# Writing the order of a feed-forward stage by hand: single steps on four engines, and some twenty turns of attention and mixing moved

## The chip, the cores and the metric

The kernel runs on one core of one Trainium2 chip. Times are device microseconds (us) of that core from launch to end. Five engines work side by side, each through its own instructions in a fixed order: TensorE (PE; its weight loads, PEld, are listed apart), VectorE (DVE), ScalarE (ACT), GpSimd (POOL), and SyncE (SP), which here only starts transfers (DMA). An instruction waits at the head of its engine's queue until what it reads has been written and the buffer that it writes is free; all that stands behind it on that engine waits with it.

## The reference, cut to what matters

```python
# attention: 8 heads, 768 tokens, head size 64; a key counts only where its hash bucket equals the query's
scores = where(q_bucket == k_bucket, q @ k.T / 8, -1e9)
x = concat_heads(softmax(scores) @ v)                    # 768 x 512
# gated feed-forward with a mixing over the tokens
h = gelu_tanh(x @ w_in)                                  # 768 x 1024
u, v = h[:, :512], h[:, 512:]
v_n = (v - mean(v)) / sqrt(var(v) + 1e-6) * g_ln
gated = u * (w_sg @ v_n + b_sg[:, None])
x = x + gated @ w_out
# eight experts, one per token (argmax of x @ w_gate, or the expert of the token before)
out[s] = p[e] * (relu(x[s] @ w1[e]) @ w2[e])
```

## The kernel before, in words

Tokens are cut into six tiles of 128. A product in full float32 is made from two halves of each factor, a rounded one ("hi") and the rest ("lo"): hi is cast by ACT or DVE, lo is a subtraction on DVE or POOL, and TensorE takes three products (hi hi, hi lo, lo hi).

**Attention** runs over the heads; the table ATTENTION writes the order of its steps for PE, DVE, ACT and POOL. `score h t` makes the scores of one query tile, `max` their row maximum (DVE, L384), `exp` the numerators (ACT, L388), `turn h i` three transposes of them into one of two PSUM banks (PE, L396), `ev h i` the copy out of that bank (ACT, L400), `pv` the product with v (PE, L410). `prep h ...` scales and splits q and k of the head two further on: `k1` is a cast (DVE, L339), `q2` a scaling (DVE, L337), `k2` a subtraction (POOL, L349). `out`, `to_x` bring a head's result to x: three transposes into bank "m" and a DVE multiplication out of it (L445). The same bank "m" takes `project` (PE, L361), which makes the hash bits of the next head. `conv` is the next of the small steps that turn w_in and w_out into hi and lo (DVE L237 to L250, a cast on ACT L256, POOL or DVE L229). `to_x 5` handles the head that the code counts as 3, since `to_x h` works on head h-2.

**Feed-forward, first stage.** h = x @ w_in comes in twelve PSUM banks: (n, t) with n = 1 for the v half and n = 0 for the u half, t the tile. Four of them (hv0 to hv3) have three quarters of their products inside the attention table. Each bank goes through gelu: Square on ACT (L641), a cubic term on DVE (L642), Tanh on ACT (L643), a product on DVE (L644). A v bank goes on: mean (DVE, L653), squared deviation (ACT, L654), z (DVE, L656), variance (DVE, L657), its power -1/2 on POOL (L658), scaling of z by it (ACT, L659), cast to hi (DVE, L660), lo (POOL, L661). Beside that stand the first two of six tiles of w_sg: a transfer, a cast on ACT (L673, `wshi`), a subtraction on POOL (L675, `wslo`).

Before, only PE's order was written out here (in the order of the code). DVE, ACT and POOL were put in order by the compiler's scheduler from its own costs.

**Mixing** follows from the table MIXING, again for four engines: `mix t k` is the k-th of 18 products of w_sg tile t with v_n, `gated t` the product with u (DVE, L686), `gT t` its transposes (PE, L692), `out t k` the product with w_out, `route t` the steps that pick experts, `w` the next step of the split of the first expert weights (ACT L614, then DVE or POOL L618). Then the **experts** run, with 4 MB of weights each; their raw buffers are six of 0.5 MB, loaded by SP as soon as one is free.

Of the kernel before, what the change touches and what calls it, by code (L numbers as in the profile page):

```python
# [67 lines left out]
turn 4 5, ev 4 5, score 4 4, max 4 4, conv 0, exp 4 4, conv 0, zero 0 4, conv 0 *3, pv 3 1, pv 3 2, turn 4 6,  # L68
ev 4 6, turn 4 7, ev 4 7, score 4 5, max 4 5, exp 4 5, project 4 1, bits 4 2, bits 4 3, sum 4 3, pv 3 3, turn 4 8,
ev 4 8, turn 4 9, ev 4 9, prep 4 k1, prep 4 k2, prep 4 hi, score 5 0, max 5 0, exp 5 0, pv 3 4, pv 3 5, turn 4 10,  # L70
ev 4 10, turn 4 11, ev 4 11, out 4, conv 0 *3, prep 4 q2, sum 5 1, prep 4 lo, fetch 5, xT 4, score 5 1, max 5 1,
exp 5 1, mean 5, low 4, turn 5 0, ev 5 0, turn 5 1, ev 5 1, score 5 2, max 5 2, exp 5 2, sum 5 0, pv 4 0,
conv 0 *4, to_x 5, turn 5 2, ev 5 2, turn 5 3, ev 5 3, score 5 3, max 5 3, exp 5 3, project 5 0, bits 5 0,
bits 5 1, pv 4 1, turn 5 4, ev 5 4, turn 5 5, ev 5 5, score 5 4, max 5 4, exp 5 4, pv 4 2, conv 0 *2, sum 5 2,
zero 0 5, turn 5 6, ev 5 6, sum 5 3, conv 0, turn 5 7, ev 5 7, score 5 5, max 5 5, exp 5 5, project 5 1, bits 5 2,
pv 4 3, turn 5 8, ev 5 8, turn 5 9, ev 5 9, score 6 0, prep 5 k1, prep 5 k2, prep 5 hi, conv 0 *2, max 6 0,
exp 6 0, pv 4 4, pv 4 5, turn 5 10, ev 5 10, turn 5 11, mean 6, ev 5 11, out 5, sum 6 0, bits 5 3, xT 5, prep 5 q2,
prep 5 lo, score 6 1, conv 0, max 6 1, low 5, exp 6 1, turn 6 0, ev 6 0, turn 6 1, ev 6 1, score 6 2, max 6 2,
exp 6 2, conv 0 *3, pv 5 0, to_x 6, sum 6 1, turn 6 2, ev 6 2, turn 6 3, ev 6 3, score 6 3, max 6 3, exp 6 3,
conv 0, pv 5 1, project 6 0, bits 6 0, bits 6 1, conv 0, turn 6 4, ev 6 4, turn 6 5, ev 6 5, sum 6 2, score 6 4,  # L80
max 6 4, exp 6 4, pv 5 2, zero 0 6, conv 0 *2, project 6 1, bits 6 2, turn 6 6, ev 6 6, turn 6 7, ev 6 7, conv 0,
score 6 5, max 6 5, exp 6 5, conv 0, bits 6 3, pv 5 3, conv 0, turn 6 8, ev 6 8, turn 6 9, ev 6 9, score 7 0,
max 7 0, exp 7 0, conv 0 *3, sum 6 3, pv 5 4, pv 5 5, out 6, turn 6 10, ev 6 10, turn 6 11, ev 6 11, sum 7 2,
mean 7, xT 6, score 7 1, max 7 1, exp 7 1, low 6, sum 7 1, turn 7 0, ev 7 0, turn 7 1, ev 7 1, score 7 2, max 7 2,
exp 7 2, sum 7 0, pv 6 0, to_x 7, conv 0, turn 7 2, ev 7 2, turn 7 3, ev 7 3, score 7 3, max 7 3, exp 7 3, pv 6 1,
# [30 lines left out]
route 2, mix 5 10, mix 5 11, route 3, mix 5 12, route 2, w 0, half 2 1, mix 5 13, gl 4, mix 5 14, route 3 *2,
mix 5 15, route 3, mix 5 16, mix 5 17, route 3, out 4 0, route 2, out 4 1, route 2, half 3 0, route 2, route 3,
out 4 2, out 4 3, out 4 4, route 3, out 4 5, out 4 6, gated 5, w 0, out 4 7, route 3 *3, out 4 8, out 4 9, w 0,
out 4 10, route 3, out 4 11, res 4, gT 5, route 3 *2, half 3 1, route 3 *2, gl 5, w 0, route 3, route 4,
route 3 *6, out 5 0, out 5 1, out 5 2, w 0, out 5 3, route 3, out 5 4, route 4, route 3, out 5 5, out 5 6, out 5 7,  # L120
route 4, out 5 8, w 0, route 4, w 0, route 4, out 5 9, out 5 10, route 4, out 5 11, res 5, gx 0 0, route 4 *2,
half 4 0, w 0, gx 0 1, route 4 *2, half 4 1, gx 1 1, gx 0 2, gx 0 3, route 5, route 4 *2, gx 1 0, gx 1 2, gx 1 3,
route 4 *2, route 5 *3, half 5 0, route 5, route 4, route 5, route 4, gx 2 0, gx 2 2, route 4, gx 2 1, route 5 *3,
w 0, route 4, route 5, route 4 *2, route 5, half 5 1, route 4 *2, route 5, gx 2 3, route 5, route 4, route 5,
route 4, gx 3 0, gx 4 0, route 4, gx 3 3, gx 4 3, gx 3 2, gx 4 2, gx 3 1, gx 4 1, route 5 *3, gx 5 0, gx 5 1,
# [20 lines left out]
def kernel(  # L146
# [480 lines left out]
    with ExitStack() as ctx_b:  # L627
# [11 lines left out]
        def gelu2(h_ps, dst, total=None):  # L639
            sq = bp2.tile([P, DM], F32, tag="sq", name="sq", bufs=3)  # L640
            nc.scalar.activation(sq, h_ps, AF.Square)  # L641
            nc.vector.scalar_tensor_tensor(sq, sq, 1.0 / A3, h_ps, op0=ALU.add, op1=ALU.mult)  # L642
            nc.scalar.activation(sq, sq, AF.Tanh, scale=CG * A3)  # L643
            nc.vector.scalar_tensor_tensor(dst, sq, 1.0, h_ps, op0=ALU.add, op1=ALU.mult, accum_out=total)  # L644
            return sq

        def v_part(t, h_ps):
            v2 = bp2.tile([P, DM], F32, tag="v2", name="v2")
            mu = bp2.tile([P, 1], F32, tag="mu", name="mu")
            var = bp2.tile([P, 1], F32, tag="var", name="var")  # L650
            rstd = bp2.tile([P, 1], F32, tag="rstd", name="rstd")
            sq = gelu2(h_ps, v2, mu)
            nc.vector.tensor_scalar_mul(mu, mu, -1.0 / DM)  # L653
            nc.scalar.activation(sq, v2, AF.Square, bias=mu, accum_out=var)  # L654
            z = bp2.tile([P, DM], F32, tag="z", name="z")
            nc.vector.scalar_tensor_tensor(z, v2, mu, gbc, op0=ALU.add, op1=ALU.mult)  # L656
            nc.vector.tensor_scalar(var, var, 1.0 / DM, 4e-6, op0=ALU.mult, op1=ALU.add)  # L657
            nc.gpsimd.tensor_tensor(rstd, var, eps4, op=ALU.pow)  # L658
            nc.scalar.activation(z, z, AF.Copy, scale=rstd)  # L659
            nc.vector.tensor_copy(vnh[:, t, :], z)  # L660
            nc.gpsimd.tensor_tensor(vnl[:, t, :], z, vnh[:, t, :].bitcast(F32), op=ALU.subtract)  # L661
# [548 lines left out]
```

## Time and profile before

| | us |
|---|---|
| median of 3 runs | 360.95 (359.12 to 362.23) |
| the profiled execution | 358.38 |
| its span | 356.6 |
| attention | 0 to about 155 |
| first feed-forward stage, first Square to last gelu | 156 to 191 |
| mixing and routing | to about 250 |
| experts | to 349 |

The profile shows one execution. An engine is busy while an instruction runs on it; idle time stands before the instruction that ended it, with the one that released it. "PEclk" is the share of full speed that the throttle granted TensorE. In the rows `out<-in` names what an instruction writes and reads.

### The profile page before, as it was taken

What the parts mean: (1) busy time and instruction counts of PE and PEld (TensorE: products, weight loads), DVE (VectorE), ACT (ScalarE), POOL (GpSimd) and SP (SyncE); (2) the same over time, 40 slices, a digit from 0 to 9 for tenths busy, and PEclk for the clock granted to TensorE, in tenths of its full rate; (3) what the DMA queues carried; (4) which work ended last, traced back from release to release, by engine and by line L of the source; (5) the groups of instructions that cost most, each with busy time, mean ns of one, the idle gap of its engine ahead of it and who ended that gap; (6) DMA issues with size and microseconds to landing.
All of it is one profiled execution on the core that took longest, in us unless ns stands there. A gap on an engine that the chain in (4) does not pass through costs nothing. (4 is left out here: it accounts for less than half of the span.)

```text
span 356.6 us, 5375 instructions
## 1 busy us (share of the span) xinstructions
PE 327.3 (92%) x1802; PEld 247.2 (69%) x1802; DVE 274.6 (77%) x553; ACT 233.2 (65%) x431; POOL 204.3 (57%) x172
## 2 busy tenths in 40 slices
PE   7678969999989999999986999997999999999990
PEld 5555546776656666688865777776888888888870
DVE  4799969887989977666875286788567989999570
ACT  3586667878868688346854465462668789978520
POOL 2457837747768534716742489597266455665351
PEclk9999999999999999999998999999999999999997
DMA  7695403213041103071012546456869999999400
GB/s 291 225 370 190 149 2 147 91 59 112 38 147 61 45 16 119 0 248 49 0 46 52 182 135 208 147 180 206 255 223 344 341 372 375 325 398 344 144 18 26
DMA packets 27535, 59.52 MB, mean 167 GB/s; under 512 B 3054, under 2 KB 7662, under 8 KB 27504
## 3 DMA queue, kind: packets, MB, share of 16 engines
q1 hardware_dynamic: 24912, 52.78, 43.5%
q0 software_dynamic: 1664, 4.74, 3.6%
q10 hardware_dynamic: 928, 1.62, 1.3%
q8 instruction: 16, 0.26, 0.3%
q14 instruction: 15, 0.12, 0.1%
HBM read 52.29 MB, written 7.36 MB: 167 GB/s over the span
## 5 line engine op out<-in xcount | busy, mean ns | idle before, releaser
L618 POOL TENSOR_TENSOR w<-raw,w 128x1024 fp32r<-128x1024 f32 x23 | 60.1, 2614 | 34.7 <-ACT w L614 34.7
L614 ACT CAST w<-raw 128x1024 fp32r<-128x1024 f32 x64 | 65.5, 1057 | 9.5 <-DMA raw<-in_w 7.7
L388 ACT ACTIVATE e<-s,nb_all 128x768 f32<-128x768 f32 x48 | 43.4, 905 | 31.6 <-DVE nb_all L384 30.8
L618 DVE TENSOR_TENSOR w<-raw,w 128x1024 fp32r<-128x1024 f32 x41 | 59.3, 1482 | 5.4 <-ACT w L614 4.4
L384 DVE TENSOR_REDUCE nb_all<-s 128x1 f32<-128x768 f32 x48 | 45.7, 953 | 11.9 <-PE s L380 11.5
L396 PEld LDWEIGHTS t<-ident,e 128*128 128x128 f32 x288 | 31.1, 140 | 27.7 <-ACT pt L400 16.9
L396 PE MATMUL t<-ident,e 128*128 128x128 f32 x288 | 42.3, 283 | 8.0 <-ACT pt L400 7.3
L400 ACT COPY pt<-t 128x384 f32<-128x384 f32 x96 | 41.2, 484 | 1.4 <-PE t L396 1.3
L410 PE MATMUL po<-pt,vt 128*64 128x384 f32 x192 | 38.1, 503 | 0.0
L968 PE MATMUL y<-w,hh 128*128 128x512 f32 x128 | 31.9, 397 | 0.4 <-DVE w L618 0.4
L377 PE MATMUL s<-k,q 128*128 128x384 f32 x96 | 28.4, 376 | 0.0
L968 PEld LDWEIGHTS y<-w,hh 128*128 128x128 f32 x128 | 23.4, 188 | 5.4 <-DVE w L618 0.8
L682 PE MATMUL vs<-vn,wshi 128*128 128x512 f32 x72 | 24.6, 417 | 1.2 <-POOL vn L661 0.9
L380 PE MATMUL s<-k,q 76*128 76x384 f32 x96 | 25.0, 342 | 0.4 <-DVE q L368 0.3
L675 POOL TENSOR_TENSOR wslo<-wsr,wshi 128x768 fp32r<-128x768 f32 x6 | 11.1, 1850 | 24.1 <-ACT wshi L673 19.2
L946 PE MATMUL eh<-w,xh 128*128 128x512 f32 x96 | 24.8, 400 | 0.0
L349 POOL TENSOR_TENSOR k<-r,k 64x768 fp32r<-64x768 f32 x7 | 13.8, 1972 | 19.1 <-DVE k L339 11.1
L270 PE MATMUL h<-w_in_s,xTs 128*128 128x512 f32 x96 | 21.9, 389 | 0.0
L410 PEld LDWEIGHTS po<-pt,vt 128*64 128x64 f32 x192 | 11.0, 135 | 14.3 <-issue 14.3
L229 POOL TENSOR_TENSOR cv_w<-cv_w,cv_a 128x512 f32<-128x512 f32 x11 | 14.3, 1299 | 11.4 <-DVE cv_w L241 11.2
L270 PEld LDWEIGHTS h<-w_in_s,xTs 128*128 128x128 f32 x96 | 18.0, 188 | 3.7
L946 PEld LDWEIGHTS eh<-w,xh 128*128 128x128 f32 x96 | 17.6, 188 | 3.8
(205 smaller groups left out, 720.2 us busy)
## 6 DMA issues: line engine op xcount, KB each, us to landing
raw<-in_w SPq DMA_DIRECT2D x64, 512.0 KB, 5.3
r<-in_qk SPq DMA_DIRECT2D x7, 768.0 KB, 4.5
raw<-in_w_in SPq DMA_DIRECT2D x8, 512.0 KB, 4.6
slots<-zt SPq DMA_DIRECT2D x7, 514.0 KB, 7.4
wsr<-in_w_sgT SPq DMA_DIRECT2D x6, 384.0 KB, 3.5
raw<-in_w_out SPq DMA_DIRECT2D x4, 512.0 KB, 3.5
xg<-slots POOLq DMA_DIRECT2D x6, 257.0 KB, 4.8
vt<-in_v_tok ACTq DMA_DIRECT2D x1, 1536.0 KB, 6.6
```

The source lines that it names most:

```text
L270: nc.tensor.matmul(ps, a[:, kc, ts_], w_in_s[:, b, kc, ns], start=(kc == 0 and i == 0), stop=(kc == 3 and i == 2))
L377: nc.tensor.matmul(s[:, j, :HALF], q1[:, ts_], k1[:, j * HALF:(j + 1) * HALF], start=True, stop=False)
L380: nc.tensor.matmul(s[:, j, :HALF], q2[:NB, ts_], k2[:NB, j * HALF:(j + 1) * HALF], start=False, stop=True)
L384: nc.vector.tensor_reduce(nb_all[:, h, t:t + 1], ss[h, t][:, :, :HALF], axis=AX.XY, op=ALU.max, negate=True)
L388: nc.scalar.activation(e, ss.pop((h, t))[:, :, :HALF], AF.Exp, bias=nb_all[:, h, t:t + 1], accum_out=rs_all[:, h, t:t + 1])
L396: nc.tensor.transpose(ps[:, i * P:(i + 1) * P], es[h, t][:, g, i * P:(i + 1) * P], ident)
L400: nc.scalar.copy(dst, tps.pop((h, t, g))[:, :HALF].rearrange("p (i q) -> p i q", i=3))
L410: nc.tensor.matmul(po[j * D:(j + 1) * D, :HALF], vt[:, kt, h * D:(h + 1) * D], pt[j][:, kt, :], start=(kt == 0), stop=(kt == NT - 1))
L614: nc.scalar.copy(hi, raw)
L618: eng.tensor_tensor(lo, raws.pop(c), hi.bitcast(F32), op=ALU.subtract)
L946: nc.tensor.matmul(ps[n], a[:, kc, :], w1s[:, b, kc * 2 + n, :], start=(k == 0), stop=(k == 11))
L968: nc.tensor.matmul(ps, a[:, kc, :], w2s[:, b, kc, :], start=(k == 0), stop=(k == 23))
```

## The change

The first feed-forward stage becomes a table like the other two. `gelu2`, `v_part` and `u_part` are cut into single steps (`h_step`), and FEED_FORWARD lists them with the four `wsg` steps. DVE, ACT and POOL take this order as written; the tiny tiles mu, var and rstd get three buffers in place of two. In ATTENTION and MIXING some twenty steps move by a place or a few. No step's operation, shape or engine changes.

```diff
 ATTENTION (some of the lines)
-score 1 0, max 1 0, exp 1 0, turn 0 10, ev 0 10, turn 0 11, ev 0 11, zero 0 0, sum_v 0 2, conv 0 *2, prep 0 q2,
-score 1 1, max 1 1, exp 1 1, sum 1 0, prep 0 k1, prep 0 k2, prep 0 lo, pv 0 0, conv 0 *2, turn 1 0, ev 1 0,
+score 1 0, max 1 0, exp 1 0, turn 0 10, zero 0 0, ev 0 10, turn 0 11, ev 0 11, sum_v 0 2, conv 0 *2, prep 0 k1,
+prep 0 q2, score 1 1, max 1 1, exp 1 1, sum 1 0, prep 0 k2, prep 0 lo, pv 0 0, conv 0 *2, turn 1 0, ev 1 0,
...
+FEED_FORWARD = """
+h 1 0, h 1 1, sq 1 0, h 1 2, cub 1 0, sq 1 1, h 1 3, cub 1 1, tanh 1 0, h 1 4, sq 1 2, gelu 1 0, tanh 1 1, cub 1 2,
...
+sq 0 4, cub 0 4, tanh 0 4, gelu 0 4, sq 0 5, cub 0 5, tanh 0 5, gelu 0 5
...
-        def gelu2(h_ps, dst, total=None):
...
+        def h_step(name, n, t):
...
+            if n:
+                for k in ("mu", "var", "rstd"):
+                    if k not in st:
+                        st[k] = bp2.tile([P, 1], F32, tag=k, name=k, bufs=3)
+            if name == "h":
+                h_mm(h_ps, t, n, (3,) if n and t < 4 else range(4))
+            elif name == "sq":
+                st["sq"] = bp2.tile([P, DM], F32, tag="sq", name="sq", bufs=3)
+                nc.scalar.activation(st["sq"], h_ps, AF.Square)
+            elif name == "cub":
+                nc.vector.scalar_tensor_tensor(st["sq"], st["sq"], 1.0 / A3, h_ps, op0=ALU.add, op1=ALU.mult)
...
-        for i in range(4):
-            h_mm(hps[i], i, 1, (3,))
-            v_part(i, hps[i])
...
+        for name, n, t in _order(FEED_FORWARD):
+            if name == "wsg":
+                wsg_tile(n, t)
+            else:
+                h_step(name, n, t)
```

PE and SP issue the same instructions in the same order as before. Three places show what moves on the others.

VectorE in attention, head 3's way to x. Before (`px` is bank "m", `s` the scores of head 5):

```order
L384 TENSOR_REDUCE nb_all<-s_2_1103 128x1
L421 RECIPROCAL rs_all<-rs_all 128x6
L250 SCALAR_TENSOR_TENSOR cv_w<-raw_876,cv_w 128x512
L237 TENSOR_SCALAR cv_a<-cv_a 128x512
L445 TENSOR_TENSOR x<-px_1120,rs_all 128x3x2x64
L384 TENSOR_REDUCE nb_all<-s_3_1136 128x1
```

and now (line numbers are 12 higher in this part):

```order
L396 TENSOR_REDUCE nb_all<-s_2_1101 128x1
L433 RECIPROCAL rs_all<-rs_all 128x6
L457 TENSOR_TENSOR x<-px_1113,rs_all 128x3x2x64
L262 SCALAR_TENSOR_TENSOR cv_w<-raw_876,cv_w 128x512
L249 TENSOR_SCALAR cv_a<-cv_a 128x512
L396 TENSOR_REDUCE nb_all<-s_3_1136 128x1
```

The multiplication that empties bank "m" now stands ahead of two steps of the weight split.

VectorE where head 3's q and k are prepared (`r` holds both as loaded). Before:

```order
L250 SCALAR_TENSOR_TENSOR cv_w<-raw_287,cv_w 128x512
L339 CAST k_3_484<-r_375 128x768
L337 TENSOR_SCALAR q_3_485<-r_375 128x768
L229 TENSOR_TENSOR w_in_s<-cv_w,w_in_s 128x512
L384 TENSOR_REDUCE nb_all<-s_0_491 128x1
```

and now:

```order
L262 SCALAR_TENSOR_TENSOR cv_w<-raw_287,cv_w 128x512
L349 TENSOR_SCALAR q_3_476<-r_375 128x768
L351 CAST k_3_475<-r_375 128x768
L241 TENSOR_TENSOR w_in_s<-cv_w,w_in_s 128x512
L396 TENSOR_REDUCE nb_all<-s_0_491 128x1
```

The cast of k, for which POOL's subtraction waits, now stands right ahead of the weight split's own subtraction. For head 2 the two are swapped the other way, and there the cast comes before a row maximum that it followed.

ScalarE at the start of the feed-forward stage. Before (`sq` with `hv` is Square, `sq<-sq` Tanh, `sq,var` the deviation, `z<-z` the scaling, `wshi` the cast of w_sg):

```order
L643 ACTIVATE sq_1758<-sq_1758 128x512
L641 ACTIVATE sq_1800<-hv2_1600 128x512
L643 ACTIVATE sq_1779<-sq_1779 128x512
L673 CAST wshi_2007<-wsr_2005 128x768
L654 ACTIVATE sq_1758,var_1756<-v2_1754,mu_1755 128x512
L643 ACTIVATE sq_1800<-sq_1800 128x512
L641 ACTIVATE sq_1821<-hv3_1601 128x512
L659 ACTIVATE z_1765<-z_1765,rstd_1757 128x512
```

and now:

```order
L673 ACTIVATE sq_1763<-sq_1763 128x512
L669 ACTIVATE sq_1798<-hv2_1600 128x512
L673 ACTIVATE sq_1772<-sq_1772 128x512
L683 ACTIVATE sq_1763,var_1752<-v2_1800,mu_1751 128x512
L673 ACTIVATE sq_1798<-sq_1798 128x512
L669 ACTIVATE sq_1814<-hv3_1601 128x512
L691 ACTIVATE z_1806<-z_1806,rstd_1753 128x512
L683 ACTIVATE sq_1772,var_1758<-v2_1811,mu_1757 128x512
L683 ACTIVATE sq_1798,var_1766<-v2_1832,mu_1765 128x512
L669 ACTIVATE sq_1845<-h1_4_1782 128x512
L704 CAST wshi_1849<-wsr_1847 128x768
```

The cast that needs a transfer stands seven instructions further on. GpSimd at the end of the stage, before (`rstd` the power, `vn` a lo half of v_n, the last one for tile 5):

```order
L675 TENSOR_TENSOR wslo_2014<-wsr_2011,wshi_2013 128x768
L658 TENSOR_TENSOR rstd_1851<-var_1850,eps4_1749 128x1
L661 TENSOR_TENSOR vn_1735<-z_1859,vn_1735 128x512
L658 TENSOR_TENSOR rstd_1882<-var_1881,eps4_1749 128x1
L661 TENSOR_TENSOR vn_1735<-z_1890,vn_1735 128x512
```

and now:

```order
L689 TENSOR_TENSOR rstd_1785<-var_1784,eps4_1749 128x1
L695 TENSOR_TENSOR vn_1735<-z_1898,vn_1735 128x512
L695 TENSOR_TENSOR vn_1735<-z_1909,vn_1735 128x512
L689 TENSOR_TENSOR rstd_1819<-var_1818,eps4_1749 128x1
L706 TENSOR_TENSOR wslo_1961<-wsr_1958,wshi_1960 128x768
L695 TENSOR_TENSOR vn_1735<-z_1954,vn_1735 128x512
```

The second subtraction of w_sg moves from ahead of tile 4's power to just ahead of tile 5's lo half.

## Rows read from the trace of the kernel before

**Rows 1.** The page, part 1: busy time of each engine, share of the span, instructions.

```profile
PE 327.3 (92%) x1802; PEld 247.2 (69%) x1802; DVE 274.6 (77%) x553; ACT 233.2 (65%) x431; POOL 204.3 (57%) x172
```

**Rows 2.** Stretches: start:end, length, busy PE PEld DVE ACT POOL, PEclk, DMA share, GB/s.

```profile
100.00:110.00 10.00, 8.92 (x54) 5.66 (x56) 8.29 (x13) 6.90 (x16) 5.56 (x8) 1.00 0.40 131
110.00:120.00 10.00, 10.00 (x68) 6.86 (x64) 9.62 (x15) 7.82 (x20) 8.21 (x8) 1.00 0.17 54
188.00:192.00 4.00, 1.19 (x8) 0.77 (x7) 2.56 (x4) 2.69 (x4) 1.32 (x1) 1.00 0.00 0
192.00:194.00 2.00, 2.00 (x7) 1.51 (x7) 1.36 (x2) 0.60 (x1) 0.50 (x1) 0.60 0.11 30
194.00:196.00 2.00, 2.00 (x7) 1.57 (x6) 1.21 (x2) 0.00 (x0) 0.00 (x0) 0.55 0.79 198
196.00:198.00 2.00, 2.00 (x10) 1.62 (x9) 0.01 (x1) 1.79 (x2) 0.91 (x1) 1.00 0.59 231
280.00:290.00 10.00, 10.00 (x52) 8.24 (x51) 8.49 (x10) 8.23 (x12) 6.31 (x4) 1.00 1.02 370
```

**Rows 3.** PE's waits from 165 to 215 us: total, times, longest.

```profile
PE gT L692 <- DVE g L686: 2.8, 1, 2.8
PE vs L682 <- POOL vn L661: 0.9, 1, 0.9
PE vs L682 <- DVE vn L660: 0.3, 1, 0.3
```

**Rows 4.** Timeline of PE in attention: start, length, what, idle time before and releaser.

```profile
34.54 0.93 PE L396 MATMUL t<-ident,e 128*128 128x128 f32 x6 [0.84 <-ACT pt L400]
46.77 0.93 PE L396 MATMUL t<-ident,e 128*128 128x128 f32 x6 [1.73 <-ACT pt L400]
101.08 0.91 PE L361 MATMUL pj<-k,wz 128*66 128x384 f32 x4 [1.78 <-DVE x L445]
```

**Rows 5.** Timeline from 97 to 101 us, DVE and POOL.

```profile
97.21 1.83 POOL L347 TENSOR_TENSOR q<-r,q 64x768 fp32r<-64x768 f32 x1
...
97.54 2.04 DVE L250 SCALAR_TENSOR_TENSOR cv_w<-raw,cv_w 128x512 uint32<-128x512 uint32 x1
...
99.51 1.05 DVE L237 TENSOR_SCALAR cv_a<-cv_a 128x512 uint32<-128x512 uint32 x1
...
100.48 0.55 DVE L445 TENSOR_TENSOR x<-px,rs_all 128x384 f32<-128x384 f32 x1
```

**Rows 6.** Timeline from 41 to 45 us, DVE and POOL.

```profile
41.23 0.55 DVE L337 TENSOR_SCALAR q<-r 128x768 fp32r<-128x768 f32 x1
41.45 2.02 POOL L349 TENSOR_TENSOR k<-r,k 64x768 fp32r<-64x768 f32 x1 [1.47 <-DVE k L339]
...
41.70 2.32 DVE L229 TENSOR_TENSOR w_in_s<-cv_w,w_in_s 128x512 fp32r<-128x512 f32 x1
...
43.94 0.94 DVE L384 TENSOR_REDUCE nb_all<-s 128x1 f32<-128x768 f32 x1
```

**Rows 7.** Timeline of POOL: the subtraction of head 2.

```profile
29.73 2.15 POOL L349 TENSOR_TENSOR k<-r,k 64x768 fp32r<-64x768 f32 x1 [1.95 <-PE t L396]
```

**Rows 8.** Timeline of the feed-forward stage: PE, ACT, POOL, DVE.

```profile
165.75 14.44 PE L270 MATMUL h<-w_in_s,xTs 128*128 128x512 f32 x63
...
161.11 0.83 ACT L673 CAST wshi<-wsr 128x768 fp32r<-128x768 f32 x1 [1.71 <-DMA wsr<-in_w_sgT]
...
176.40 1.85 POOL L675 TENSOR_TENSOR wslo<-wsr,wshi 128x768 fp32r<-128x768 f32 x1 [0.52 <-ACT wshi L673]
176.47 2.33 DVE L656 SCALAR_TENSOR_TENSOR z<-v,mu,gbc 128x512 f32<-128x512 f32 x1
```

**Rows 9.** Timeline of the stage's last turns on DVE.

```profile
184.57 0.68 DVE L642 SCALAR_TENSOR_TENSOR sq<-sq,h 128x512 f32<-128x512 f32 x1
...
190.51 0.75 DVE L686 SCALAR_TENSOR_TENSOR g<-vs,bsg,u 128x512 f32<-128x512 f32 x1
```

**Rows 10.** SP's waits before issuing a weight load: total, times, longest.

```profile
SPq L611 <- POOL w L618: 52.3, 21, 7.0
```

More of the change, by code (lines that the diff above doesn't have):

```diff
@@ L67 @@
 turn 4 3, ev 4 3, score 4 3, sum 4 2, max 4 3, exp 4 3, project 4 0, bits 4 1, bits 4 0, turn 4 4, ev 4 4,
[L68 to L85, printed above, removed]
+turn 4 5, ev 4 5, score 4 4, max 4 4, conv 0 *2, exp 4 4, zero 0 4, conv 0 *3, pv 3 1, pv 3 2, turn 4 6, ev 4 6,
@@ new lines @@
+pv 5 0, to_x 6, sum 6 1, turn 6 2, ev 6 2, turn 6 3, ev 6 3, score 6 3, max 6 3, exp 6 3, conv 0, pv 5 1,
+project 6 0, bits 6 0, conv 0, bits 6 1, turn 6 4, ev 6 4, turn 6 5, ev 6 5, sum 6 2, score 6 4, max 6 4, exp 6 4,
+pv 5 2, zero 0 6, conv 0 *2, project 6 1, bits 6 2, turn 6 6, ev 6 6, turn 6 7, ev 6 7, conv 0, score 6 5, max 6 5,
+exp 6 5, conv 0, bits 6 3, pv 5 3, conv 0, turn 6 8, ev 6 8, turn 6 9, ev 6 9, score 7 0, max 7 0, exp 7 0,
+conv 0 *3, sum 6 3, pv 5 4, pv 5 5, out 6, turn 6 10, ev 6 10, turn 6 11, ev 6 11, sum 7 2, mean 7, xT 6,
@@ L116 @@
[L116 to L125, printed above, removed]
@@ L126 @@
-route 5 *5, gx 5 2, gx 5 3, route 5 *3, w 0
+mix 5 3, mix 5 4, mix 5 5, mix 5 6, route 2 *3, half 2 0, mix 5 7, route 3, gT 4, mix 5 8, mix 5 9, route 2,
+mix 5 10, mix 5 11, route 3, mix 5 12, route 2, w 0, half 2 1, mix 5 13, gl 4, mix 5 14, route 3 *2, mix 5 15,
+route 3, mix 5 16, mix 5 17, route 3, out 4 0, route 2, out 4 1, route 2, half 3 0, route 2, route 3, out 4 2,
+out 4 3, out 4 4, route 3, out 4 5, out 4 6, gated 5, w 0, out 4 7, route 3 *3, out 4 8, out 4 9, w 0, out 4 10,
+route 3, out 4 11, res 4, gT 5, route 3 *2, half 3 1, route 3 *2, gl 5, w 0, route 3, route 4, route 3 *6, out 5 0,
@@ L570 @@
     ctx_o.close()
-    ctx_o.enter_context(tc.manual_schedule(engines={ET.PE}))
+    ctx_o.enter_context(tc.manual_schedule(engines={ET.PE, ET.DVE, ET.Activation, ET.Pool}))
     slab2 = ctx.enter_context(tc.tile_pool(name="slab2", bufs=1, reuse_waits="tile"))
@@ L637 @@
         nc.vector.memset(eps4, -0.5)
-        def gelu2(h_ps, dst, total=None):
[L640 to L661, printed above, removed]
@@ L854 @@
         gx = []
-        ctx_o.close()
-        ctx_o.enter_context(tc.manual_schedule(engines={ET.PE, ET.DVE, ET.Activation, ET.Pool}))
         PARTS = ("h0", "l0", "h1", "l1", "h2", "l2", "h3", "l3")
```

91 lines of the change are left out of this document (69 added, 22 removed).

## The prediction

> **What bounds the kernel now.** The page first: PE is busy for 92% of the span, more than any other engine [rows 1]. So I looked for the places where PE is not busy, since only there can an order of steps give time back. PE's waits from 165 to 215 us add up to 4.0 us, all at the end of the first feed-forward stage: 0.9 and 0.3 us for the last tile of v_n, then 2.8 us for `gated 0` [rows 3]. [...] In attention three of PE's waits stand where the change moves something [rows 4].
>
> **Why the stage ends late.** Its work for ACT, DVE and POOL has three marks of a poor order. ACT stands 1.71 us for a transfer, ahead of a cast whose reader, `mix 0`, cannot begin before 180 us [rows 8]. A z took 2.33 us on DVE while POOL's `wslo` ran beside it for 1.85 us [rows 8]; an operation of its kind and size takes 0.75 [rows 9]. And the last three tiles run one at a time: Square, cubic term, Tanh and product follow each other between ACT and DVE, so that 184.57 to 190.51 is three turns of 1.98 us [rows 9].
>
> **The change, term by term** (times against the profiled execution, 358.38 us; the median of the runs shown, 360.95, is 2.57 higher, and the forecast goes by that median).
>
> *First feed-forward stage.* PE has the same instructions as before. It ends the products of h at 180.2 (165.75 + 14.44) at 14.44/63 = 0.229 us each [rows 8]. Up to `gT 0` stand 18 + 11 products of `mix`, so PE can be there at 180.2 + 29 x 0.229 = 186.9, if v_n is ready in time; it was there at 191.3 (188.5 + 2.8). I laid the new order out by hand with the durations of the rows (an estimate): each engine in its order, and a z or a cast on DVE and a POOL operation one after the other where they meet. The cast of w_sg no longer stands before the first deviation, which is then some 2.6 us earlier; tile 5's z ends at about 177.2; its scaling begins at 179.0. `wslo 1` now runs there and holds tile 5's cast to hi until 180.8. The cubic terms of tiles 2 and 3 of u stand close together, so that only tiles 4 and 5 run one at a time: they begin at about 183.0 and take 2 x 1.98. `gated 0` then starts at 187.0 and ends at 187.8, where it ended at 191.3. The last lo half is there at 182.5; PE asks for it at 180.2 + 16 x 0.229 = 183.9, so the waits of 0.9 and 0.3 go as well (they are inside the 4.4 that PE can win). Late next is `gated 0` still, by 0.9 us. **Gain 3.5.** Ends: 4.4, if PE never waits; a loss of 1.2, if three more operations of the tail pay 1.6 us each (2.33 - 0.75) for POOL. I take 3.5, since the layout already charges such meetings.
>
> *The clock.* From 192 to 196 us PE lost 2 x 0.40 + 2 x 0.45 = 1.7 us [rows 2]. With one wait of 0.9 in place of 4.0 in all, the nearest row is the wait of 1.78 us at 101 us, whose stretch shows a granted clock of 1.00 [rows 2, 4]. **Gain 1.7**; ends 0 and 1.7.
>
> *Head 3's multiplication.* PE stood 1.78 us for bank "m" [rows 4], because the multiplication waited behind two steps of the weight split, of which one took 2.04 us beside POOL's 1.83 [rows 5]. It now stands ahead of both; its transposes are done long before. PE may lose nothing there. What is queued behind it, the two split steps, becomes 0.5 us later, and the row maximum after them stays where it was or a little earlier. **Gain 1.5**; ends 0 and 1.78. [...] The rows that bear on it: from 110 to 120 us PE is busy for 10.00, its weight loads for 6.86 and DVE for 9.62 of 10 us [rows 2]. DVE is nearly as full as PE there; but in the 10 us before it was busy for 8.29 only, so it can start earlier too, and I keep 1.5.
>
> *Head 3's q and k.* The row maximum at 43.94 stood behind a split step of 2.32 us that waited for POOL's subtraction (2.02) [rows 6]; the exponential and the evictions behind it made PE wait 1.73 us at 46.77 [rows 4]. Now the split step follows the cast at once and can go ahead of POOL, as the scaling at 41.23 did. The split step then ends at about 42.4 (41.78 + 0.7), and the maximum begins there, not at 43.9; POOL's subtraction becomes some 0.8 us later, and its chain ends well before its reader. **Gain 1.6**; ends 0 and 1.73.
>
> *Head 2's q and k, the other way.* The cast (as long as head 3's scaling, 0.55 [rows 6]) delays the scaling and a maximum; POOL's subtraction of 2.15 us [rows 7] starts about 1 us earlier, and what waited for it is freed earlier, ahead of PE's wait of 0.84 [rows 4]. **0**; ends a gain of 0.5 and a loss of 2.1, if POOL's subtraction gets in between.
>
> *The rest.* SP's order is unchanged, so the moved `fetch` and `zero` steps cost nothing. A cast of the weight split now precedes one exponential of head 4 and waits for DVE: evictions cover it, and without that cover it costs less than the 0.83 us of a larger cast [rows 8]. The other moves swap neighbours on engines that wait for PE; the later copies for routing and third buffers of tiny tiles have no reader near. **0**; ends 0 and a loss of 0.8.
>
> Sum: 3.5 + 1.7 + 1.5 + 1.6 = 8.3. From 358.38 that gives 350.1; from the median, **352.7**.
>
> **Does it reach the end?** Mixing starts from `gT 0` on every engine, and the wait of SP for weight buffers (52.3 us for POOL's subtractions alone [rows 10]) says that loads are asked for by this order, not by a clock of their own. So what PE wins, the loads win.
>
> **The rivals.**
>
> *The tail of the stage stays late, the rest comes true.* Meetings of DVE and POOL fall out worse, and `gated 0` ends near 190; the clock still falls for a while. The stage gives 1.3, the clock 0.5, attention 2.7: 360.95 - 4.5 = 356.5. For it: the prices in rows 8. Against: those meetings are in the layout. Chance 0.22.
>
> *The weights set the end.* In the experts DMA is full: 370 GB/s and a share of 1.02 from 280 to 290 us [rows 2]. If the loads did not start earlier, 8 us would shrink to at most what the stretch before them gives, and the time would be about 360. [...] Rows 10 and the DMA share of 0.00 from 188 to 192 us [rows 2] speak against: loads stop when buffers are full. Chance 0.14.
>
> *Slower.* ACT, now fixed in order, stands at the scalings of z until POOL's power is there; all later Squares and Tanhs queue behind. Before, the scheduler had put other work between. If each of tiles 3, 4 and 5 loses 2.3 us there (one `vl` or `wslo` more than laid out), `gated 0` ends at 187.8 + 6.9 = 194.7, 3.4 later than before; PE then waits about 8 us and loses clock for longer, some 2 us more; less 3 from attention: 360.95 + 2.4 = 363.4. It decides when `gated 0` ends after 194. For it: two z rows of three quarters and more above their length. Against: it needs three such losses. Chance 0.05.
>
> The forecast itself has 0.59. About 1% (3.6 us) is what a measurement of this kernel can tell from no change. The forecast and most of the first rival lie more than that below 360.95: faster 0.59 + 0.19 = 0.78. The weights' rival and the rest of the first: same 0.17. Slower 0.05. The range goes from 350.0, the ends of all gains taken (3.5 and 1.6 grown to 4.4 and 1.73, 1.78 at bank "m", 0.5 at head 2: 10.1, with a little of the spread between runs), to 358.5, which takes in the first rival with its attention gain halved; the likeliest case's own range is 350 to 355.
>
> **What would show it.** In the changed profile: PE waits less than 0.3 us at the projection near 100 us and at the turn near 46; no cast of w_sg waiting for a transfer before the first deviation; `gated 0` ending some 3.5 us closer to that stage's first Square than before; PE waiting about 1 us in the stage; a granted clock of 1.00 behind it; the experts as long as before. The forecast is wrong if PE's wait at `gT 0` is over 2 us, if PE shows new waits between 47 and 100 us that eat the gains, or if the experts grow by what the front wins.

## The result, and the profile after

The changed kernel takes **350.28 us** (median of 4, 349.02 to 351.70). The kernel before, run beside it, took 361.31; the ratio is 0.970, 95% interval 0.965 to 0.976. The forecast was 352.7 with a range from 350.0 to 358.5, so the time lies 0.3 above the range's lower end.

The profiled execution of the changed kernel took 350.61 us (span 348.7). PE is busy for a little longer than before in a span 7.9 us shorter. From the page, part 1, against [rows 1]:

```profile
PE 328.2 (94%) x1802; PEld 250.0 (72%) x1802; DVE 270.7 (78%) x553; ACT 233.5 (67%) x431; POOL 203.6 (58%) x172
```

A span alone does not say which edit earned what. So I took the start times of a few PE instructions that each trace has, and compared the stretches between them. "One table back" is the changed kernel with MIXING as it was (experiment 10); its profile shows a granted clock of 1.00 from 16 to 240 us. Two of the eight runs of experiment 3 were slow, the profiled one (362.39 us) among them: its ratio leaves them out, and of its trace only the stretch from 53 to 157 us, at a granted clock of 1.00, is set against others.

| stretch, us | before | changed | one table back | gain, before to changed | forecast |
|---|---|---|---|---|---|
| start to a turn of head 0 | 26.08 | 28.26 | 26.21 | -2.18 | 0 |
| to the next products of bank "m" | 24.95 | 22.64 | 22.60 | 2.31 | 1.6 + 0 (heads 3, 2) |
| to the projection near 100 us | 50.05 | 48.11 | 48.13 | 1.94 | 1.5 |
| to the stage's first Square | 55.33 | 55.37 | 55.38 | -0.04 | 0 |
| to `gT 0` | 34.91 | 30.20 | 30.20 | 4.71 | 3.5 |
| to the first x2T (mixing) | 8.53 | 6.95 | 6.94 | 1.58 | 1.7 (clock) |
| to the first xgT (experts) | 63.74 | 63.69 | 63.74 | 0.05 | 0 |
| to the end of the span | 93.01 | 93.48 | 93.80 | -0.47 | 0 |

All four gains are there; the loss in the first row needs a look. The stretches of the changed kernel, with busy PE, PEld, DVE, ACT, POOL, then PEclk, DMA share and GB/s, answer to [rows 2]:

```profile
16.00:20.00 4.00, 4.00 (x15) 3.54 (x16) 1.23 (x2) 2.73 (x7) 2.46 (x3) 0.50 1.03 382
28.00:32.00 4.00, 3.74 (x15) 2.05 (x15) 4.00 (x6) 2.93 (x8) 3.37 (x3) 0.62 0.81 279
100.00:110.00 10.00, 10.00 (x64) 6.31 (x61) 9.63 (x14) 8.66 (x21) 7.31 (x10) 1.00 0.50 164
...
188.00:192.00 4.00, 4.00 (x21) 3.25 (x21) 1.35 (x2) 1.79 (x2) 0.94 (x1) 1.00 0.75 219
192.00:194.00 2.00, 2.00 (x19) 1.27 (x17) 0.07 (x1) 1.19 (x2) 2.00 (x2) 1.00 0.01 2
194.00:196.00 2.00, 2.00 (x14) 1.66 (x11) 1.45 (x7) 0.54 (x4) 1.24 (x1) 1.00 0.69 194
...
280.00:290.00 10.00, 10.00 (x50) 8.24 (x49) 9.11 (x9) 7.38 (x10) 5.17 (x4) 1.00 1.01 368
```

Three things are to be seen. PE is busy for 4.00 of the 4 us from 188 to 192, where before it stood for `gated 0` and was busy for 1.19 (it comes to that step 6.7 us earlier now: 184.58 against 191.32). The clock behind the stage is 1.00. And from 16 to 32 us this execution shows 0.50 to 0.73 in places, where the profile of before shows 1.00: that is the 2.18 us of the first row. The trace of one table back has 1.00 there and 26.21 us, so the new order does not bring it by itself. Without it the two spans differ by 356.6 - 347.0 = 9.6 us.

PE in the changed kernel where [rows 3, 4] had its waits (a row with no bracket waited for nothing):

```profile
46.39 0.93 PE L408 MATMUL t<-ident,e 128*128 128x128 f32 x6
...
99.01 0.85 PE L373 MATMUL pj<-k,wz 128*66 128x384 f32 x4
...
184.58 0.60 PE L723 MATMUL gT<-ident,g 128*128 128x128 f32 x4
```

The stage itself: ACT's cast of w_sg, POOL's subtractions, three casts on DVE, z and scaling of tile 5 and the last turns on DVE, against [rows 8, 9]:

```profile
161.89 0.82 ACT L704 CAST wshi<-wsr 128x768 fp32r<-128x768 f32 x1
163.79 1.85 POOL L706 TENSOR_TENSOR wslo<-wsr,wshi 128x768 fp32r<-128x768 f32 x1
163.93 1.99 DVE L693 CAST vn<-z 128x512 fp32r<-128x512 f32 x1 [0.52 <-ACT z L691]
...
166.63 0.95 DVE L693 CAST vn<-z 128x512 fp32r<-128x512 f32 x1
...
172.99 0.74 DVE L686 SCALAR_TENSOR_TENSOR z<-v,mu,gbc 128x512 f32<-128x512 f32 x1
...
175.36 1.85 POOL L706 TENSOR_TENSOR wslo<-wsr,wshi 128x768 fp32r<-128x768 f32 x1
175.43 0.73 ACT L691 ACTIVATE z<-z,rstd 128x512 f32<-128x512 f32 x1 [0.20 <-POOL rstd L689]
176.19 1.30 DVE L693 CAST vn<-z 128x512 fp32r<-128x512 f32 x1 [0.23 <-ACT z L691]
...
179.40 0.68 DVE L671 SCALAR_TENSOR_TENSOR sq<-sq,h 128x512 f32<-128x512 f32 x1
...
181.38 0.68 DVE L671 SCALAR_TENSOR_TENSOR sq<-sq,h 128x512 f32<-128x512 f32 x1
...
183.43 0.74 DVE L717 SCALAR_TENSOR_TENSOR g<-vs,bsg,u 128x512 f32<-128x512 f32 x1
```

The cast no longer waits for its transfer, `gated 0` ends at 183.43 + 0.74 = 184.17, and PE asks for it at 184.58: the stage's wait is gone with 0.4 us to spare. Both of POOL's subtractions of w_sg still meet a cast on DVE, and a lo half of v_n meets a third: the casts took 1.99, 1.30 and 0.95, where three others of the kind took 0.42.

### The profile page after: what moved, and what is told of

Its sections match the earlier page's. It is cut to its first block, busy times and chain, and to the rows that moved or that the text cites. A ratio compares the mean times of both kernels' runs of the same rounds, so it can differ in the third digit from the quotient of the medians.

```text
span 348.7 us, 5379 instructions
## 1 busy us (share of the span) xinstructions
PE 328.2 (94%) x1802; PEld 250.0 (72%) x1802; DVE 270.7 (78%) x553; ACT 233.5 (67%) x431; POOL 203.6 (58%) x172
## 5 line engine op out<-in xcount | busy, mean ns | idle before, releaser
L630 POOL TENSOR_TENSOR w<-raw,w 128x1024 fp32r<-128x1024 f32 x23 | 59.2, 2576 | 36.3 <-ACT w L626 34.6
L626 ACT CAST w<-raw 128x1024 fp32r<-128x1024 f32 x64 | 65.4, 1057 | 10.1 <-DMA raw<-in_w 8.9
L408 PEld LDWEIGHTS t<-ident,e 128*128 128x128 f32 x288 | 32.6, 144 | 23.9 <-ACT pt L412 15.1
L408 PE MATMUL t<-ident,e 128*128 128x128 f32 x288 | 43.5, 289 | 4.6 <-ACT pt L412 3.9
L389 PE MATMUL s<-k,q 128*128 128x384 f32 x96 | 29.5, 389 | 0.0
L392 PE MATMUL s<-k,q 76*128 76x384 f32 x96 | 25.8, 351 | 0.3 <-DVE q L380 0.3
L713 PE MATMUL vs<-vn,wshi 128*128 128x512 f32 x72 | 23.7, 406 | 0.0
L392 PEld LDWEIGHTS s<-k,q 76*128 76x128 f32 x96 | 18.2, 198 | 0.9 <-issue 0.6
```

The source lines that it names most:

```text
L389: nc.tensor.matmul(s[:, j, :HALF], q1[:, ts_], k1[:, j * HALF:(j + 1) * HALF], start=True, stop=False)
L392: nc.tensor.matmul(s[:, j, :HALF], q2[:NB, ts_], k2[:NB, j * HALF:(j + 1) * HALF], start=False, stop=True)
L408: nc.tensor.transpose(ps[:, i * P:(i + 1) * P], es[h, t][:, g, i * P:(i + 1) * P], ident)
L626: nc.scalar.copy(hi, raw)
L630: eng.tensor_tensor(lo, raws.pop(c), hi.bitcast(F32), op=ALU.subtract)
```

## The experiments

The reasons on trial: the feed-forward order and the attention order add up; within the first, the place of the w_sg steps; within the second, one swap or move for each wait; and whether PE's wait at `gT 0` brings the lowered clock.

**1 and 2. Either table alone.** The kernel before with the new feed-forward order, ATTENTION and MIXING as they were; and the kernel before with the new ATTENTION only.

> The kernel before with the feed-forward table alone; ATTENTION and MIXING as before. Theory (terms add up): the stage's last gelu and gated 0 end about 29.8 us after the stage's first Square in place of 34.9, PE has no wait at gT 0, the granted clock is 1.00 behind it; 4.4 + 1.7 = 6.1 us faster than the kernel before. Rival (the tables only work together, the order of the feed-forward needs the earlier arrival of attention): PE still waits 1 us or more at gT 0 and the gain is under 4 us.

> The kernel before with the ATTENTION table of the change alone. Theory: PE's waits at 46.8 us (1.73) and at bank m near 101 us (1.78) go, about 3.5 us faster up to the feed-forward stage, which keeps its wait of 2.8 us at gT 0 and its lowered clock: 3 to 4 us faster in all. Rival (PE's wait only moves on, since VectorE is nearly full from 110 to 120 us): under 2 us.

Feed-forward alone: 354.88 us (ratio 0.979, 0.974 to 0.985), so 6.0 less than the 360.92 of before beside it. First Square to `gT 0` takes 30.20 us, as in the whole change, and no wait is left; the two waits of attention, 1.73 and 1.78, are still there. Attention alone: 356.23 us (0.985, 0.980 to 0.991), 4.7 less, more than expected; its first Square comes 4.45 us earlier (151.96 against 156.41), where 3.5 were expected. 6.0 + 4.7 = 10.7 of the 11.0 by which the medians of the whole differ: within the spread of these runs, some 2 us for each, the parts add. Up to the experts the traces say the same: attention alone takes 22.58, 48.11 and 55.39 us for the stretches from the turn to the first Square, as the whole change does (22.64, 48.11 and 55.37).

In the experts they do not. There the profiled execution of attention alone took 96.84 us (from xgT at 257.66 to 354.5) against 93.01 before, and gave back 3.8 of the 5.9 us that it was ahead at x2T. Three subtractions of the weight split on DVE took 7.07 us beside two of POOL's, where before three took 3.50 (from 262.63), and PE waited for the step queued behind them:

```profile
256.70 7.07 DVE L618 TENSOR_TENSOR w<-raw,w 128x1024 fp32r<-128x1024 f32 x3 [1.76 <-ACT w L614]
...
264.54 1.20 PE L946 MATMUL eh<-w,xl 128*128 128x512 f32 x4 [1.66 <-DVE xl L936]
```

One thing did not come. Attention alone keeps the stage's wait, and its clock behind it stays at 1.00, as its stretches show:

```profile
184.00:186.00 2.00, 0.17 (x1) 0.00 (x0) 1.30 (x3) 1.14 (x2) 0.00 (x0) 1.00 0.00 0
186.00:188.00 2.00, 1.07 (x7) 0.98 (x8) 0.87 (x2) 1.53 (x3) 1.71 (x1) 1.00 0.00 0
188.00:190.00 2.00, 2.00 (x11) 1.60 (x10) 1.75 (x3) 0.22 (x1) 0.12 (x1) 1.00 0.15 39
```

**3. Head 3's multiplication alone**, in the kernel before:

```diff
-sum 5 0, pv 4 0, conv 0 *4, to_x 5, turn 5 2
+sum 5 0, pv 4 0, to_x 5, conv 0 *4, turn 5 2
```

> The kernel before with one move alone: head 3's multiplication out of bank m ahead of four steps of the weight split. Theory: no wait of PE at the projection near 101 us, and the feed-forward stage's first Square begins 1.8 us earlier (at about 154.6). [...]

360.03 us (median of eight; ratio 0.995, 0.990 to 1.000). The difference in time is too small for these runs, so the trace decides: from the products of bank "m" to the projection 48.13 us (53.82 to 101.95) against 50.05 before, so 1.92 won, and up to the first Square 1.84 of it is kept. (The first Square itself was expected at about 154.6 us and came at 157.36.) The multiplication now stands right behind the products, and PE's projection row has no wait (timeline, DVE and PE):

```profile
100.65 0.56 DVE L445 TENSOR_TENSOR x<-px,rs_all 128x384 f32<-128x384 f32 x1 [0.22 <-PE px L443]
101.13 1.27 DVE L250 SCALAR_TENSOR_TENSOR cv_w<-raw,cv_w 128x512 uint32<-128x512 uint32 x1
...
101.95 0.86 PE L361 MATMUL pj<-k,wz 128*66 128x384 f32 x4
```

The split step took 1.27 us where it had taken 2.04 [rows 5]: it now begins 1.1 us into POOL's subtraction (100.03 to 101.85) and meets only the end of it.

**4. Head 3's q and k alone**, in the kernel before:

```diff
-prep 1 hi, prep 1 k1, prep 1 k2, prep 1 q2, ev 1 9
+prep 1 hi, prep 1 q2, prep 1 k1, prep 1 k2, ev 1 9
```

> The kernel before with one swap alone: head 3's scaling of q ahead of its cast of k on VectorE. Theory: the weight split's subtraction runs before GpSimd's subtraction in place of after it and takes about 0.7 us in place of 2.3; the row maximum behind it starts 1.4 us earlier; PE's wait of 1.73 us near 46.8 shrinks below 0.4; at the next head's transposes of x near 51 us about 0.3 us of it are given back. [...]

359.72 us (0.994, 0.992 to 0.997). The split step takes 0.68 where it took 2.32 [rows 6], the maximum follows at once, and the wait of 1.73 is gone; from the turn ahead of it (46.26; 43.46 before) to bank "m" it takes 5.99 us in place of 7.57, so 1.58 us are won (timeline, DVE and POOL):

```profile
44.50 0.68 DVE L229 TENSOR_TENSOR w_in_s<-cv_w,w_in_s 128x512 fp32r<-128x512 f32 x1
44.72 2.15 POOL L349 TENSOR_TENSOR k<-r,k 64x768 fp32r<-64x768 f32 x1 [1.95 <-DVE k L339]
45.10 0.95 DVE L384 TENSOR_REDUCE nb_all<-s 128x1 f32<-128x768 f32 x1
```

**5. A wait of the old kind put back.** The changed kernel, with more work for DVE ahead of `gated 0`:

```diff
-sq 0 5, cub 0 5, tanh 0 5, gelu 0 5
+sq 0 5, cub 0 5, tanh 0 5, gelu 0 5 *6
```

> The changed kernel with the last product of gelu of tile 5 of the u half written six times instead of once (the same values again; the extra five are the only added work): VectorE reaches gated 0 five products later, 5 x 0.61 = about 3.05 us. Question: what does a wait of the old kind at gT 0 cost, and does it bring the lowered clock behind it? Theory 1 (the prediction's clock term): PE waits 3.05 - 0.4 (gated 0 ended 0.4 us before PE asked for it) = about 2.6 us at gT 0 and the granted clock falls between 186 and 196 us below 0.7 for about 4 us; the time is 350.3 + 2.6 + 1.7 = 354.6. Theory 2: the fall belongs to some executions and not to the wait (the kernel with the new attention order alone had a wait of 2.8 us and a granted clock of 1.00 behind it): the clock stays 1.00 and the time is 350.3 + 2.6 = 352.9. Rival to both: the experts are set by weight loads and take the wait back: 350.3 to 351.

353.71 us (353.01 to 355.96), 3.4 above the changed kernel, between the two theories. In the profile the fall is there; the stretches behind the stage:

```profile
184.00:186.00 2.00, 0.62 (x3) 0.62 (x4) 1.33 (x3) 1.29 (x3) 0.02 (x1) 0.86 0.00 0
186.00:188.00 2.00, 2.00 (x8) 1.61 (x7) 0.68 (x2) 1.29 (x2) 1.80 (x1) 0.50 0.00 0
188.00:190.00 2.00, 2.00 (x8) 1.60 (x7) 1.85 (x3) 0.00 (x0) 0.00 (x0) 0.78 0.37 106
```

and PE's wait before it, with the first x2T:

```profile
185.38 1.09 PE L723 MATMUL gT<-ident,g 128*128 128x128 f32 x4 [3.09 <-DVE g L717]
...
193.96 0.60 PE L747 MATMUL x2T<-ident,x 128*128 128x128 f32 x4
```

From `gT 0` to x2T it took 193.96 - 185.38 = 8.58 us, where the changed kernel takes 6.95: 1.63 for the clock, beside the wait of 3.09. From the first Square to the end it is 5.14 us longer (351.4 - 151.94 against 348.7 - 154.38), and the two together are 4.72: in this pair a wait here reaches the end of the kernel whole, and the experts take nothing of it back (93.71 us against 93.48).

**6. The cast of w_sg back ahead of the first deviation**, and **7. the second tile of w_sg back ahead of tile 4's power**, each in the changed kernel:

```diff
-dev 1 0, z 1 0, tanh 1 2, ... cub 1 3, sq 1 4, wsg 0 0, var 1 2
+wsg 0 0, dev 1 0, z 1 0, tanh 1 2, ... cub 1 3, sq 1 4, var 1 2
```
```diff
-h 0 2, var 1 4, ... tanh 0 1, wsg 1 0, sq 0 2, var 1 5, gelu 0 0, wsg 1 1, gelu 0 1
+h 0 2, wsg 1 0, wsg 1 1, var 1 4, ... tanh 0 1, sq 0 2, var 1 5, gelu 0 0, gelu 0 1
```

> The changed kernel with one step put back: the first cast of w_sg stands ahead of the first deviation again, where it stood before the change. Theory (the prediction's account of the stage): ACT stands 1.5 to 2 us for the transfer there, all deviations, Squares and Tanhs behind it are later, gated 0 ends 1 to 2 us later against the first Square (29.8 us now) and PE waits 0.6 to 1.6 us at gT 0 or for the last tile of v_n: 351 to 352. Rival: the place of that cast matters little, because the stage's gain comes from the order of the last tiles: gated 0 ends within 0.4 us of 29.8 and the time stays at 350.3.

> The changed kernel with the second tile of w_sg (cast on ACT, subtraction on POOL) moved from behind tile 5's variance to ahead of tile 4's, which is where POOL did that subtraction before the change. This tries the mechanism of the slower rival once: POOL's 1.85 us then stand ahead of tile 4's power, ACT stands at tile 4's scaling until the power is there, and all later Squares and Tanhs queue behind it. Theory: the power of tile 4 comes up to 1.85 us later and a z on VectorE pays about 1.5 us for the meeting with POOL; gated 0 ends 1.5 to 2.5 us later against the first Square (29.8 us now) and PE waits 1.1 to 2.1 us at gT 0: 351.5 to 352.5. Rival: ACT has other work that covers it (the cast itself moves too) and the last tiles set the end: within 0.4 us of 29.8, no wait, 350.3.

The first: 351.88 us. ACT waits 1.27 for the transfer, `gated 0` ends 31.55 us after the first Square instead of 29.79, and PE waits 1.26 (timeline, ACT and PE):

```profile
157.53 0.83 ACT L704 CAST wshi<-wsr 128x768 fp32r<-128x768 f32 x1 [1.27 <-DMA wsr<-in_w_sgT]
...
184.88 0.66 PE L723 MATMUL gT<-ident,g 128*128 128x128 f32 x4 [1.26 <-DVE g L717]
```

The second: 351.53 us. Here ACT stands at the scalings for POOL's power, as the slower rival had it; but no z pays for POOL's subtraction, which the theory had too (they take 0.74 to 0.75); `gated 0` ends 31.36 us after the first Square, and PE waits 1.06 (timeline, POOL, ACT and PE):

```profile
169.91 1.85 POOL L706 TENSOR_TENSOR wslo<-wsr,wshi 128x768 fp32r<-128x768 f32 x1 [1.56 <-ACT wshi L704]
...
172.31 0.73 ACT L691 ACTIVATE z<-z,rstd 128x512 f32<-128x512 f32 x1 [1.46 <-POOL rstd L689]
...
176.18 0.72 ACT L691 ACTIVATE z<-z,rstd 128x512 f32<-128x512 f32 x1 [0.92 <-POOL rstd L689]
...
184.26 0.66 PE L723 MATMUL gT<-ident,g 128*128 128x128 f32 x4 [1.06 <-DVE g L717]
```

The two places account for 1.8 and 1.6 of the 5.1 us by which `gated 0` ends closer to the first Square (34.85 before), if they add; that was not tried. The rest, 1.7, had no experiment of its own. Near it in size is the third mark that the prediction names: only two turns run one at a time now, where there were three of 1.98 each. The traces carry both verdicts: the medians stand 1.60 and 1.25 us above the changed kernel's, and their runs overlap with its own.

**8. Two more waits of attention attacked**, in the changed kernel: 1.46 us at the turn at 28.26, and 1.23 at bank "m":

```diff
-conv 0 *2, bits 0 3, sum 1 2, prep 0 hi, sum_v 0 1, turn 0 8, ev 0 8, turn 0 9, ev 0 9,
+turn 0 8, ev 0 8, turn 0 9, ev 0 9, conv 0 *2, bits 0 3, sum 1 2, prep 0 hi, sum_v 0 1,
...
-pv 1 0, sum 2 0, to_x 2, turn 2 2, ev 2 2, turn 2 3, ev 2 3
+pv 1 0, sum 2 0, turn 2 2, ev 2 2, turn 2 3, to_x 2, ev 2 3
```

> The changed kernel with two moves more, aimed at the waits that PE still shows in attention: 1.46 us at the turn at 28.26 us (for an eviction on ACT) and 1.23 us for bank m at 50.90 us (for ACT's step on the mean of v). First: turns and evictions 8 and 9 of head 0 go ahead of the small split steps, the sum and the preparation that stood before them. Second: to_x 2 goes behind two turns and one eviction. Theory (a wait of PE ahead of the feed-forward stage is worth its length, as for head 3): both waits go, 350.3 - 1.4 - 1.1 = 347.8. Rivals: only one of the two goes, 349; or a wait of the same length appears at the next turn, 350.3; or the moved evictions delay the split steps or the q and k of head 2 so that the next score waits for them, 351 to 352.

350.51 us (347.83 to 352.63): by the median nothing is won, and the runs are too far apart to tell 1 us. The trace says why so little could be. Both waits are smaller, and PE is no earlier behind them. Against experiment 6, which has the attention order of the change and nearly the same clock there, the turn near 32.2 us starts 0.10 later, bank "m" 0.11 later, and the projection near 56.4 us 0.06 earlier. Short waits stand in between; 0.50 and 0.21 are new, the one of 0.96 is in experiment 6 too (at 32.11). The profiled run was the slowest of the six: its mixing took 1.35 us longer and its experts 1.9 longer than the changed kernel's, so it says nothing on the end (timeline of PE):

```profile
28.89 0.86 PE L422 MATMUL po<-pt,vt 128*64 128x384 f32 x2 [0.50 <-ACT pt L412]
...
32.21 0.93 PE L408 MATMUL t<-ident,e 128*128 128x128 f32 x6 [0.96 <-ACT pt L412]
...
49.83 0.55 PE L455 MATMUL px<-ident,ot 128*128 128x128 f32 x3 [0.41 <-ACT vmean L478]
...
54.96 0.93 PE L408 MATMUL t<-ident,e 128*128 128x128 f32 x6 [0.21 <-ACT pt L412]
```

**9. Head 2's q and k in the old order**, in the changed kernel, and **10. the old MIXING** in the changed kernel:

```diff
-prep 0 k1, prep 0 q2, score 1 1, max 1 1, exp 1 1, sum 1 0, prep 0 k2
+prep 0 q2, score 1 1, max 1 1, exp 1 1, sum 1 0, prep 0 k1, prep 0 k2
```

> The changed kernel with head 2's q and k back in the old order (scaling first, cast of k later). The prediction had this swap at 0, between a gain of 0.5 and a loss of 2.1. Theory: 350.3 +- 0.5, with the time between the turn at 24 us and the product of bank m at 50 us the same within 0.3 us. Rival 1: the swap is what removed the old wait of 0.84 us or shifted 1.2 us into bank m's wait: that stretch differs by 0.5 us or more.

> The changed kernel with the mixing table of before. The prediction had those moves at 0. Theory: 350.3 +- 0.5, and from the transposes of gated 0 to the first product of the experts the same as now (184.58 to 255.22, 70.64 us) within 0.3 us. Rival: the moved route, half and w steps are worth up to 0.8 us there: 70.9 us or more.

349.24 and 349.53 us (two runs each). By time neither can be told from the changed kernel. Their traces have a granted clock of 1.00 from 16 to 240 us and the same turn at 26.20 and 26.21, so they can be laid side by side. Head 2 in the old order (timeline, POOL, DVE and PE):

```profile
29.84 2.14 POOL L361 TENSOR_TENSOR k<-r,k 64x768 fp32r<-64x768 f32 x1 [1.95 <-PE t L408]
...
30.23 2.03 DVE L249 TENSOR_SCALAR cv_a<-cv_a 128x512 uint32<-128x512 uint32 x1
...
34.64 0.93 PE L408 MATMUL t<-ident,e 128*128 128x128 f32 x6 [0.84 <-ACT pt L412]
...
49.55 0.55 PE L455 MATMUL px<-ident,ot 128*128 128x128 f32 x3 [1.01 <-ACT vmean L478]
```

and in the new one (experiment 10):

```profile
28.46 2.02 POOL L361 TENSOR_TENSOR k<-r,k 64x768 fp32r<-64x768 f32 x1 [0.55 <-issue]
...
30.95 1.06 DVE L249 TENSOR_SCALAR cv_a<-cv_a 128x512 uint32<-128x512 uint32 x1
...
34.38 0.93 PE L408 MATMUL t<-ident,e 128*128 128x128 f32 x6
...
48.81 0.55 PE L455 MATMUL px<-ident,ot 128*128 128x128 f32 x3 [1.21 <-ACT vmean L478]
```

With the old order the split step pays for POOL (2.03 for 1.06) and the wait of 0.84 [rows 4] is back; bank "m" is 0.74 us later. So head 2's swap is worth 0.74 and not nothing: rival 1 holds. It is kept up to the first Square (153.07 and 152.32); the spans are alike all the same (346.9 and 347.0), since experiment 10 took 0.8 us longer in the experts. From `gT 0` to the experts the old MIXING takes 70.68 us, the new one 70.64: up to there those moves are worth nothing, as forecast.

## Why the prediction was right, point by point

The likeliest case came true, in its places; the sizes were off in both directions. That the time fell inside the range is in part luck: the medians differ by 11.0 us where 8.3 were forecast, more than all the ends taken together (10.1), and only the allowance for the spread of the runs took it in.

*First feed-forward stage, 3.5: measured 4.71.* This is the term that was mis-sized most. Where the prediction said "late next is `gated 0` still, by 0.9 us", PE is late next and `gated 0` is 0.4 early. The layout by hand had tile 5's z end at 177.2 and its scaling begin at 179.0, which is 20.8 and 22.6 us after the first Square; they came at 19.35 and 21.05. The two turns at the end took 1.98 and 2.05 (179.40, 181.38, 183.43), where 1.98 each was laid out. So nearly all of the error lies ahead of the end of tile 5's z. Which step the layout had too long there is not on record and stays open. It was not that meetings of DVE with POOL went away: they cost DVE 2.98 us in three casts now (1.99, 0.95 and 1.30 for 0.42), and 2.71 us before, in two z (1.47, and 2.33 in [rows 8], for 0.75) and a cast (0.83 for 0.42):

```profile
162.94 1.47 DVE L656 SCALAR_TENSOR_TENSOR z<-v,mu,gbc 128x512 f32<-128x512 f32 x1
...
170.12 0.83 DVE L660 CAST vn<-z 128x512 fp32r<-128x512 f32 x1 [0.77 <-ACT z L659]
```

They fell on other steps: no z paid for one (all six took 0.74 to 0.75). So the second of the three marks of a poor order changed its place and did not go. What went is a mark that the prediction does not name: ACT stood 5.8 us at the scalings of z for POOL's power before, and stands 0.8 us there now (ACT's waits from 153 to 193 us: total, times, longest; before, then changed):

```profile
ACT z L659 <- POOL rstd L658: 5.8, 6, 1.6
...
ACT z L691 <- POOL rstd L689: 0.8, 3, 0.5
```

What that is worth by itself was not tried, nor were the third buffers of mu, var and rstd, which came with the new order; in experiment 7, where ACT stands 3.0 us there, `gated 0` is 1.6 us later. The end given as "if PE never waits", 4.4, was the case, and PE's own chain was 0.3 us shorter than 0.229 us a product made it.

*The clock, 1.7: measured 1.58, and its reason holds only in part.* The changed kernel has no wait and no fall. But the fall is not a fixed price of the wait, as the sum took it. From `gT 0` to x2T:

| execution of | PE's wait at `gT 0` | `gT 0` to x2T |
|---|---|---|
| before | 2.81 | 8.53 |
| before, head 3's q and k swapped | 2.79 | 8.54 |
| changed, `gated 0` made late | 3.09 | 8.58 |
| before with the new ATTENTION | 2.76 | 6.98 |
| changed, w_sg steps moved (6, 7) | 1.26, 1.06 | 7.00, 6.99 |
| changed; feed-forward alone | none | 6.95; 6.94 |

Of four executions with a wait of 2.8 to 3.1 us, three paid 1.58 to 1.63 behind it and one paid nothing (0.03); none with up to 1.26 did. So 1.58 is right for the profiled pair, and the mean of the four is 1.2. The clock may still be worth more than that over all executions. The mean granted clock of whole runs was 0.965 to 0.991 in the 19 runs of before beside experiments 1 to 4 (mean 0.980), and 0.977 to 0.994 in the four of the changed kernel (mean 0.987). The profiled run of before had 0.990, so it lost less than most. This goes the way of the 11.0 us between the medians, against 9.6 between the two traces with little loss; where the clock fell in the other runs is not known.

*Head 3's multiplication, 1.5: measured 1.92 alone and 1.94 in the change*, above its end of 1.78; where the other 0.14 us came from was not followed. That DVE is nearly as full as PE from 110 to 120 us (9.62 and 10.00 of 10 us [rows 2]) did not hold the gain back: in the changed kernel DVE is busy for 9.63 of 10 us from 100 to 110 us already, and up to the first Square PE kept all but 0.04 to 0.08 us of what it won.

*Head 3's q and k, 1.6: measured 1.60* (from the turn at 26.2 us to bank "m", 24.95 before and 49.55 - 26.20 = 23.35 with head 2 in the old order), and 1.58 alone. (41.78 + 0.7 is 42.5 and not 42.4; the term does not hang on it.)

*Head 2's swap, 0: measured 0.74*, beyond its upper end of 0.5. The prediction saw that POOL's subtraction would start about 1 us earlier, but priced neither the split step that then no longer meets it, nor the wait of 0.84 as gone.

*The rest, 0.* It is 0 up to the experts; these took 0.5 us longer in the changed kernel and 0.8 in experiment 10. That is within what executions differ by: in ten of the twelve profiles the experts took 93.0 to 93.8 us, in experiment 8 95.4, in attention alone 96.8. So "what PE wins, the loads win" held for the changed kernel, but not for every execution.

With the clock at 1.00 from 16 to 32 us, 1.60 + 0.74 + 1.92 + 4.71 + 1.59 - 0.8 = 9.8, beside the 9.6 between the spans; -0.1 and -0.05 stand in the other rows. The forecast was 8.3.

*The rivals.* The tail is not late. The slower rival's mechanism exists (experiment 7 shows it, 1.06 us of PE for one such step) but the order as written avoids it. Its sentence that before "the scheduler had put other work between" is wrong: it was the kernel before that stood at the scalings, for 5.8 us. No run has a wait of 8 us at `gT 0`, so the 2 us of clock in its sum were the author's estimate; behind the longest wait there, 3.09 us, it was 1.63. The weights do not set the end of the changed kernel: of the 8.3 us won up to x2T 0.4 were given back, although the DMA share is 1.01 from 280 to 290 us. The loads moved forward with the work: SP issued the last load of expert weights at 320.6 us, and at 328.9 before. Where much was given back (attention alone, 3.8 of 5.9 us), the waits that PE's rows show are for DVE.

## What to carry to other kernels

Look for a wait of the engine that sets the end, and ask which one instruction its releaser queued behind; moving that instruction, or the one that it queued behind, by a few places was worth 0.7 to 1.9 us, as long as PE's own work was what came next. Where the releaser itself waits for another engine, as ACT between 24 and 50 us here (5.3 us for DVE's row maxima in the changed kernel), a wait moved away can come back a step later (0.50 and 0.21 us in experiment 8). When DVE and POOL share work, order the long POOL operation so that DVE's next operations are already under way (a split step took 0.69 us when it began 0.2 us ahead of POOL's subtraction, 2.32 when it began 0.25 us behind it) or not of a kind that it holds up (the row maximum in experiment 4 took its usual 0.95 us beside POOL's subtraction). And read a gain through to the last stage: experts of the same order took from 93.0 to 96.8 us.
